# RWKV-7 recurrence and feed-forward: y's and the state's products as one of 104 columns

## The chip, the cores and the metric

The kernel runs on one core of a Trainium2 chip. What is measured is the device time of one launch in microseconds. All data is fp32.

The engines are called as the profile calls them: PE is TensorE's matmul, PEld its weight load, DVE is VectorE, ACT is ScalarE, POOL is GpSimd, SP is SyncE, which here issues nearly all DMA transfers.

## The reference

A linear recurrence over 768 steps for 4 batches of 8 heads, with a state of 40x40 for each head, and then a feed-forward block with a hard-swish:

```python
for t in range(S):                      # B, H, S, D = 4, 8, 768, 40
    y[:, :, t] = np.einsum('bhd,bhde->bhe', rt, state)
    Sa = np.einsum('bhde,bhe->bhd', state, at)
    state_decay = state * wt[:, :, None, :] - np.einsum('bhd,bhe->bhde', Sa, bt)
    state = state_decay + np.einsum('bhd,bhe->bhde', vt, kt)
...
x = attn_out.transpose(0, 2, 1, 3).reshape(B * S, H * D)     # 3072 x 320
h = x @ w_in                                                  # 320 x 2048
g = h * np.clip(h + 3.0, 0.0, 6.0) / 6.0
return g @ w_out                                              # 2048 x 320
```

The kernel takes the recurrence by blocks of 64 steps. Within a block the outputs come from the state at its start and from masked scores among its own steps; the correction Sa is found by inverting a triangular 64x64 matrix for each head.

## The kernel before

A *unit* is two batches by 64 steps by 8 heads; there are 24, numbered from 0. Units with even and odd numbers hold different batches, so unit i + 2 is the next that works on unit i's state. The 128 partitions hold two halves of 64: the two batches of a unit (q) or two heads (s). Four units form a group, for which VectorE inverts the triangular matrices in some 60 small steps (`invert`, L738 and L744).

A unit has two sets of stages. The *preparation* (`prepare`) needs no state: W and gam (running products of the decay), A, B, K (transposes and scaling), F (the matrix to invert), factor (scaled k and b, the tile KBt, held as `o["K"]` and `o["B"]`), E (masked scores of k and a) and EV (E times v). The unit's *own* stages (`step`) are:

- RT, VT: transposes of r and v; RT also scales the state by the decay
- R (L853): state times a, plus EV; S: transposes of the state; C: scores of v and r, masked
- U (L891), UT (L911): minus the inverse times R, as it is and transposed; rS (L927): the part of y from the old state, kept in ys
- sn (L946): the state's products, K's columns by v and B's columns by U, summed in PSUM, and then added to the state (L954, two instructions of VectorE); H: scores of U and r, masked
- y (L969): K's columns by C and B's columns by H, summed in PSUM, added to ys (L980), then multiplied by gam on POOL (L981, yg)
- move, move2: eight DMA transfers of yg into xt, the feed-forward's input

sn and y load the same columns of K and B as weights (40 of a head for sn, 64 for y). Each is 32 matmuls on quarters of the array, and each fp32 matmul leaves two records in the profile.

`masked` (L517) copies scores from PSUM into one of three score tiles through a 0/1 mask; the rest of such a tile stays zero. C, H and E take the three tiles in turn. U has a tile of its own, whose columns 40 to 63 of every head POOL clears for each unit (L868). That tile's place is also used by K1, an input tile of the odd units among the first eight.

The first four units follow a plan written by hand (`PLAN`). From unit 4 on the order is that of *blocks*, four to a unit: `OWN_STAGES` gives the own stages of unit i for the blocks from 4(i - 4) on, so its last two lists fall into the first two blocks of the next unit; `AHEAD_STAGES` or `CLOSE_STAGES` gives those of a unit whose preparation begins about five units earlier (`CLOSE_STAGES` where the next preparation begins less than four blocks later, units 8 to 11). `together` issues a block: first the TensorE products of all its stages, in the order of `PRODUCTS`, then what the other engines do with them, in the order of `RESULTS`. It counts PSUM banks as it goes (five to a batch); `WIDTH` gives the columns that a stage takes of a bank pair, and stages share a pair up to 512 columns. Feed-forward pieces (`feed`, `pieces`; L1051 and L1092 on TensorE, L1066 on ACT and L1067 on VectorE) and steps of the inversion (`aside`) come in between.

V is fetched into one of five tiles (L452, on SP's queue); the fetch waits for the last reader of the unit five before.

```python
OWN_STAGES = [["RT", "VT"], ["R", "C", "S"], ["U", "UT", "rS"], ["sn", "H"], ["y"],
              ["move", "move2"]]
AHEAD_STAGES = [["W", "gam"], ["A", "B"], ["F", "K"], ["E", "factor"], ["EV"]]
CLOSE_STAGES = [["W", "gam"], ["A", "B"], ["F", "K", "factor"], ["E"], ["EV"]]
```

Of the kernel before, what the change touches and what calls it, by code (L numbers as in the profile page):

```python
# [16 lines left out]
P = 128  # L17
BL = 64
HB = BL // 2
L = 32  # L20
SLOT = 64
EXP = 916

# [7 lines left out]
def kernel(  # L31
# [161 lines left out]
    def second(name):  # L193

        tag = {"B": "S", "K": "U"}[name]
        return padded(grp.tile([P, H, SLOT], F32, name=name + "1", tag=tag, bufs=1), name)

# [13 lines left out]
    for t in wms:  # L211
        nc.vector.memset(t[:], 0.0)
    inputs, others = {}, {}
    for name in "WABK":
# [4 lines left out]

    score = []  # L220
    for i in range(3):
        t = const.tile([P, H, BL], F32, name=f"score{i}")
        nc.gpsimd.memset(t[:], 0.0)
        score.append(t)
    turn = [0]
# [273 lines left out]
    def half(i, n=SLOT):  # L499
        return slice(SLOT * i, SLOT * i + n)  # L500

    def scores(lhs, rhs, swap=False):


        o = ps_pair(NPR, BL)
        for n in range(NPR):
            for q in range(2):
                for i in range(2):
                    nc.tensor.matmul(out=o[i][half(q), n, :],  # L509
                                     lhsT=lhs[half(i, D), n ^ (2 * q * swap), half(q)],  # L510
                                     rhs=rhs[half(i, D), n, half(q)], start=True, stop=True)
        return o

    def masked(o):
        turn[0] += 1
        x = score[turn[0] % len(score)]
        nc.vector.copy_predicated(out=x[:].rearrange("p (i h) t -> p i h t", i=2), mask=mask8, data=o[2])  # L517
        return x


    def prepare(i, F):
# [158 lines left out]
        def ev_stage():  # L680
# [8 lines left out]
            yield PE  # L689
            EV = grp.tile([P, 2, NPR, D], F32, name="EV", tag="EV")  # L690
            for x in range(2):
# [125 lines left out]
    def step(i):  # L817
# [47 lines left out]

        def new_U():
            U = m["U"] = grp.tile([P, H, SLOT], F32, name="U", tag="U", bufs=1)
            nc.gpsimd.memset(U[:, :, D:SLOT], 0.0)  # L868

        def s_S():  # L870

            sp = ps_any([P, 2, 2, P])
            for q in range(2):
                for j in range(2):
                    nc.tensor.transpose(out=sp[:, q, j, :],  # L875
                                        in_=st[:, q, 2 * j:2 * j + 2, :].rearrange("p r d -> p (r d)"),
                                        identity=ident[:])
            yield PE
            S = m["S"] = grp.tile([P, 2, 2, P], F32, name="S", tag="S", bufs=1)
            nc.scalar.activation(out=S[:], in_=sp[:], func=AF.Copy)  # L880
            new_U()

        def s_U():

            if fresh:
                new_U()
            up = ps_pair(NPR, D)
            for pr in range(NPR):
                for s in range(2):
                    for x in range(2):  # L890
# [3 lines left out]
            yield PE  # L894
            nc.scalar.activation(out=m["U"][:].rearrange("p (x r) d -> p x r d", x=2)[:, :, :, 0:D], in_=up[2],
                                 func=AF.Copy, scale=-1.0)

        def s_C():
            x = scores(m["VT"], m["RT"])
            yield PE  # L900
            m["K"] = masked(x)

# [33 lines left out]
        def s_sn():  # L936
            wide = SLOT if i < NU else D
            sn = ps_pair(NPR, D)
            for name in "KB":
                for pr in range(NPR):  # L940
                    for s in range(2):
                        for q in range(2):
# [3 lines left out]
                            nc.tensor.matmul(  # L946
                                out=sn[q][half(s, wide), pr, :],
                                lhsT=o[name][half(q), h * D:h * D + wide], rhs=by,
                                start=(name == "K" and pr == 0), stop=(name == "B" and pr == NPR - 1),
                            )  # L950
            yield PE
            for rows in [slice(0, P)] if i < NU else [half(s, D) for s in range(2)]:
                x = st[rows, :, :, 0:D]
                nc.vector.tensor_tensor(out=x, in0=sn[2][rows], in1=x, op=ALU.add)  # L954

        def s_H():
            x = scores(m["UT"], m["RT"], swap=True)
            yield PE
            m["B"] = masked(x)

# [37 lines left out]
        def s_move2():  # L998
            for dst, src in m["moves"][4:]:
# [5 lines left out]
                "rS": s_rS,  # L1005
                "sn": s_sn, "H": s_H, "y": s_y, "move": s_move, "move2": s_move2}

# [294 lines left out]
    for _ in range(18):  # L1302
# [6 lines left out]

    OWN_STAGES = [["RT", "VT"], ["R", "C", "S"], ["U", "UT", "rS"], ["sn", "H"], ["y"],  # L1310
                  ["move", "move2"]]
    AHEAD_STAGES = [["W", "gam"], ["A", "B"], ["F", "K"], ["E", "factor"], ["EV"]]
    CLOSE_STAGES = [["W", "gam"], ["A", "B"], ["F", "K", "factor"], ["E"], ["EV"]]


    PRODUCTS = ["W", "S", "K", "RT", "VT", "A", "B", "factor",
                "y", "EV", "R", "C", "U", "UT", "rS", "sn", "H", "E", "F"]
    RESULTS = ["RT", "y", "W", "VT", "EV", "R", "S", "C", "A", "B", "move", "move2",
               "U", "UT", "rS", "F", "K", "sn", "H", "E", "factor", "gam"]
    TURNS = PRODUCTS[:3]  # L1320
    WIDTH = {"R": NPR * D, "U": NPR * D, "sn": NPR * D, "EV": NPR * D}
    BLOCKS = 4
# [61 lines left out]
    def feed(n, inversion):  # L1384
# [5 lines left out]
        pieces(n - whole)  # L1390

    m = 0
    for i in range(NU, NK):
# [60 lines left out]
```

## Time and profile before

| | us |
|---|---|
| median of 3 runs | 800.2 |
| lowest and highest | 797.25, 800.67 |
| the profiled execution, device time | 800.17 |
| the profiled execution, span from first to last instruction | 798.4 |
| PE busy in the span | 734.0 |
| feed-forward on PE: L1051, L1092 | 252.6, 230.2 |
| sn on PE, L946 (both halves), 768 + 768 records | 14.4 + 14.0 |
| y on PE, L969 (last three places in PSUM), 1472 records | 27.4 |
| EV on PE, L687, 704 records | 14.9 |
| DVE state additions, L954, 44 | 21.4 |
| POOL clearings of U, L868, 24 of 0.256 | 6.1 |

The span is what the profile sees, from the first instruction to the last; the device time also holds what lies around it. A group of the profile is named by line, engine, operation, written and read tiles, and the sizes of both; its busy time is the union of its instructions, which overlap on PE. A line can be that of a helper: L509 is `scores`, called by E, C and H, and L517 is `masked`.

### The profile page before, as it was taken

To read this page: it belongs to the slowest core of one execution; us is meant where nothing else is said; L and a number is where in the kernel's file an instruction comes from. 1 tells how busy PE (TensorE), PEld (TensorE's weight loads), DVE (VectorE), ACT (ScalarE), POOL (GpSimd) and SP (SyncE) were. 2 spreads that over 40 slices of the span, in tenths; PEclk is the share of its full clock that TensorE was granted. 3 is DMA by queue.
4 is the path that set the end of the run, shared out by engine and by line. 5 is a ranking of instruction groups with operands and counts; after the bars stand their busy time and mean duration, and the time that the engine had idled before them with its cause. 6 is when DMAs were issued, how large, how long until landed. Compare 5 with 4: busy or idle time off the path is not lost.

```text
span 798.4 us, 35296 instructions
## 1 busy us (share of the span) xinstructions
PE 734.0 (92%) x15832; PEld 624.0 (78%) x15832; DVE 500.5 (63%) x986; ACT 307.1 (38%) x648; POOL 177.1 (22%) x318
## 2 busy tenths in 40 slices
PE   5726778999999989999999999999999999999998
PEld 4625667878778878788888888888888888888886
DVE  7898877689546699445798355888444983323210
ACT  2337653222553424452334454334444324412111
POOL 6403012421223313123214123304222202000000
PEclk9855798999999999999999999999999999999999
DMA  9693653420324322233212223213222101110000
GB/s 122 113 202 87 155 140 55 78 46 9 57 51 72 62 44 39 44 62 59 45 40 42 49 54 63 50 30 62 40 51 45 24 16 29 30 25 13 14 19 17
DMA packets 174214, 45.02 MB, mean 56 GB/s; under 512 B 157424, under 2 KB 172784, under 8 KB 174064
## 3 DMA queue, kind: packets, MB, share of 16 engines
q1 hardware_dynamic: 169760, 42.03, 27.8%
q8 instruction: 125, 2.05, 1.1%
q10 hardware_dynamic: 4304, 0.74, 0.7%
q14 instruction: 25, 0.20, 0.1%
HBM read 34.08 MB, written 3.93 MB: 48 GB/s over the span
## 4 chain that ended last, share of the span: by engine, by line
PE 77%; DVE 8%; issue 5%; SPq 5%; DMA 3%; ACT 1%; POOL 1%; POOLq 0%; DVEq 0%; ACTq 0%
PE h L1051 27%; PE o L1092 23%; PE pair L509 4%; PE pair L969 3%; SPq L455 3%; PE one L471 2%; PE pair L946 2%; PE pair L481 2%; PE pair L853 2%; PE pair L891 2%; PE pair L687 1%; PE pair L911 1%; PE pair L927 1%; PE one L875 1%; SPq L452 1%
## 5 line engine op out<-in xcount | busy, mean ns | idle before, releaser
L1051 PE MATMUL h<-xt,win 128*128 128x128 f32 (+1 forms) x2304 | 252.6, 284 | 3.2 <-DVE gt L1067 2.7
L1051 PEld LDWEIGHTS h<-xt,win 128*128 128x128 f32 (+1 forms) x2304 | 232.9, 193 | 20.6 <-issue 5.4
L1092 PE MATMUL o<-wout,gt 128*128 128x320 f32 x768 | 230.2, 443 | 0.0
L1092 PEld LDWEIGHTS o<-wout,gt 128*128 128x128 f32 x768 | 138.3, 190 | 50.2
L1067 DVE SCALAR_TENSOR_TENSOR gt<-gt,h 128x512 f32<-128x512 f32 x96 | 62.0, 682 | 71.2 <-ACT gt L1066 71.0
L1066 ACT ACTIVATE gt<-h,three 128x512 f32<-128x512 f32 x96 | 62.2, 686 | 101.6 <-PE h L1051 101.2
L981 POOL TENSOR_TENSOR yg<-ys,gam 128x512 f32<-128x512 f32 x22 | 39.7, 1803 | 162.6 <-DVE ys L980 71.8
L738 DVE TENSOR_TENSOR prod<-x 128x30 f32<-128x30 f32 (+9 forms) x180 | 67.2, 373 | 8.8 <-POOL x L723 3.3
L660 POOL TENSOR_TENSOR KBt<-K,rgt 128x320 f32<-128x320 f32 x22 | 19.1, 866 | 212.3 <-ACT rgt L649 207.4
L744 DVE TENSOR_TENSOR x<-x,prod 128x30 f32<-128x30 f32 (+9 forms) x180 | 62.3, 346 | 5.4
L954 DVE TENSOR_TENSOR state<-pair,state 40x320 f32<-40x320 f32 (+1 forms) x44 | 21.4, 487 | 65.5 <-PE pair L946 39.2
L517 DVE COPY_PREDICATED score<-mask,pair 128x512 f32<-128x512 int32 x71 | 50.0, 723 | 1.7 <-PE pair L509 1.2
L980 DVE TENSOR_TENSOR ys<-pair,ys 128x512 f32<-128x512 f32 x22 | 15.2, 690 | 40.9 <-PE pair L687 21.7
L552 DVE TENSOR_TENSOR_SCAN wm<-wm,start 128x528 f32<-128x528 f32 x24 | 37.6, 1566 | 0.8
L541 DVE TENSOR_TENSOR_SCAN prods<-wm,start 128x528 f32<-128x528 f32 x24 | 30.1, 1260 | 10.2 <-ACT wm L538 10.1
L831 ACT ACTIVATE RT<-pair 128x512 f32<-128x512 f32 x21 | 12.5, 597 | 52.8 <-PE pair L481 52.7
L692 ACT ACTIVATE EV<-pair 64x320 f32<-64x320 f32 x44 | 19.0, 432 | 33.7 <-PE pair L687 23.1
L806 ACT ACTIVATE tinv<-pair 32x256 f32<-32x256 f32 x48 | 18.0, 375 | 30.1 <-PE pair L796 29.4
L569 POOL COPY gam<-prods 128x256 f32<-128x256 f32 x24 | 22.5, 938 | 30.6 <-DVE prods L541 26.7
L1110 ACT ACTIVATE ob<-o 128x320 f32<-128x320 f32 x22 | 9.6, 435 | 49.4 <-PE o L1092 29.6
L969 PE MATMUL pair<-score,KBt 64*64 64x64 f32 x1472 | 27.4, 221 | 1.1 <-DVE state L954 0.9
L969 PEld LDWEIGHTS pair<-score,KBt 64*64 64x64 f32 x1472 | 24.0, 134 | 3.7 <-DVE state L954 1.4
(262 smaller groups left out, 1061.6 us busy)
## 6 DMA issues: line engine op xcount, KB each, us to landing
V<-in_v_dram SPq DMA_DIRECT2D x96, 40.0 KB
out_dram<-ob SPq DMA_DIRECT2D x47, 80.0 KB
R<-in_r_dram SPq DMA_DIRECT2D x92, 40.0 KB
B<-in_b_dram SPq DMA_DIRECT2D x42, 80.0 KB
K<-in_k_dram SPq DMA_DIRECT2D x42, 80.0 KB
W<-in_w_dram SPq DMA_DIRECT2D x37, 80.0 KB
A<-in_a_dram SPq DMA_DIRECT2D x37, 80.0 KB
xt<-yg SPq DMA_DIRECT2D x72, 40.0 KB
```

Source lines behind the costliest of these rows:

```text
L509: nc.tensor.matmul(out=o[i][half(q), n, :], lhsT=lhs[half(i, D), n ^ (2 * q * swap), half(q)], rhs=rhs[half(i, D), n, half(q)], start=True ...
L517: nc.vector.copy_predicated(out=x[:].rearrange("p (i h) t -> p i h t", i=2), mask=mask8, data=o[2])
L541: nc.vector.tensor_tensor_scan(out=prods[:].rearrange("p r m i -> p (r m i)"), data0=wm[:, 0:SCAN], data1=start[:], initial=0.0, op0=ALU.m ...
L552: nc.vector.tensor_tensor_scan(out=back, data0=back, data1=start[:], initial=0.0, op0=ALU.mult, op1=ALU.add)
L738: nc.vector.tensor_tensor(out=pv, in0=_ap(x[:], (i + 1) * L + i, [[L, n], [0, i]]), in1=_ap(x[:], i * L, [[0, n], [1, i]]), op=ALU.mult,)
L744: nc.vector.tensor_tensor(out=rest, in0=rest, in1=pv, op=ALU.add)
L969: nc.tensor.matmul(out=y[q][half(s), pr, :], lhsT=o[name][half(q), h * D:h * D + SLOT], rhs=m[name][half(q), 4 * rs + 2 * s + j, :], start ...
L981: nc.gpsimd.tensor_tensor(out=yg[:], in0=m["ys"][:].rearrange("p r q t -> p r (q t)"), in1=o["G"][:], op=ALU.mult)
L1051: nc.tensor.matmul(out=hp[c][:, i, :], lhsT=lhsT, rhs=rhs, start=(begun[c] == 0), stop=(begun[c] == 3 * NQ - 1))
L1066: nc.scalar.activation(out=gt[:], in_=hp[c][:], func=AF.Relu, bias=three[:], scale=1.0)
L1067: nc.vector.scalar_tensor_tensor(out=gt[:], in0=gt[:], scalar=6.0, in1=hp[c][:], op0=ALU.min, op1=ALU.mult)
L1092: nc.tensor.matmul(out=op[:], lhsT=gts[c][:, n, :], rhs=wout[:, c * HJ + r * NQ + n, :], start=((split or r == 0) and c == 0 and n == 0), ...
```

## The change

From unit 4 on, sn is no longer a stage of its own. y's products get a moving operand of 104 columns: 64 of masked scores and, beside them, 40 of v (for K's columns) or of U (for B's). The result holds y in its first 64 columns and the state's products in the other 40; VectorE adds the first to ys, then the second to the state. Two views of a new tile `store` hold the operands: `by_v` and `by_u`. C's and H's masks are written into them, ACT writes U beside H, and a new stage, beside, copies v beside C by a DMA transfer from SBUF to SBUF on SP's queue. H's scores are taken in another order of heads, so that H and U stand in the same order.

Three slots of `store` serve the first four units as score tiles and as the place of U and K1; U's columns 40 to 63 are no longer cleared for each unit. From unit 4 on only one score tile is left, for E. EV moves from the block after E to four blocks after E (two in `CLOSE_STAGES`), and has four slots instead of five.

```diff
+    store = const.tile([P, 2 * H * BOTH], F32, name="store")
+    slots = [store[:, n * H * BL:(n + 1) * H * BL].rearrange("p (h t) -> p h t", h=H) for n in range(3)]
+    by_v, by_u = (store[:, n * H * BOTH:(n + 1) * H * BOTH].rearrange("p (h t) -> p h t", h=H) for n in range(2))
...
-    score = []
-    for i in range(3):
-        t = const.tile([P, H, BL], F32, name=f"score{i}")
-        nc.gpsimd.memset(t[:], 0.0)
-        score.append(t)
+    score = [const.tile([P, H, BL], F32, name="score")[:], slots[0], slots[1]]
+    for t in score:
+        nc.gpsimd.memset(t, 0.0)
...
-    def scores(lhs, rhs, swap=False):
+    def scores(lhs, rhs, swap=False, back=False):
...
-                                     rhs=rhs[half(i, D), n, half(q)], start=True, stop=True)
+                                     rhs=rhs[half(i, D), n ^ (2 * q * back), half(q)],
+                                     start=True, stop=True)
...
+    def masked_beside(o, x):
+        nc.vector.copy_predicated(out=x[:, :, 0:BL].rearrange("p (h i) t -> p i h t", i=2), mask=mask8, data=o[2])
+        return x
...
-            EV = grp.tile([P, 2, NPR, D], F32, name="EV", tag="EV")
+            EV = grp.tile([P, 2, NPR, D], F32, name="EV", tag="EV", bufs=NU)
...
-        def new_U():
-            U = m["U"] = grp.tile([P, H, SLOT], F32, name="U", tag="U", bufs=1)
-            nc.gpsimd.memset(U[:, :, D:SLOT], 0.0)
...
+            m["U"] = by_u[:, :, BL:] if halves else slots[2][:, :, 0:D]
...
-            m["K"] = masked(x)
+            m["K"] = masked_beside(x, by_v) if halves else masked(x)
...
+            x = scores(m["UT"], m["RT"], swap=not halves, back=halves)
+            yield PE
+            m["B"] = masked_beside(x, by_u) if halves else masked(x)
+
+        def s_beside():
+
+            nc.sync.dma_start(out=by_v[:, :, BL:], in_=VN[:, :, 0:D])
+            yield from ()
+
+        def s_y_sn():
+
+            y = ps_pair(NPR, BOTH)
+            for name in "KB":
+                for pr in range(NPR):
+                    for s in range(2):
+                        for q in range(2):
+                            h = 2 * pr + s
+                            x = 4 * s + pr if name == "K" else 4 * (s ^ q) + pr
+                            nc.tensor.matmul(
+                                out=y[q][half(s), pr, :],
+                                lhsT=o[name][half(q), h * D:h * D + SLOT], rhs=m[name][half(q), x, :],
+                                start=(name == "K" and pr == 0), stop=(name == "B" and pr == NPR - 1))
+            yield PE
+            yg = m["yg"] = tmp.tile([P, NPR, P], F32, name="yg", tag="yg", bufs=2)
+            x = m["ys"][:].rearrange("p r q t -> p q r t")
+            nc.vector.tensor_tensor(out=x, in0=y[2][:, :, :, 0:BL], in1=x, op=ALU.add)
+            nc.gpsimd.tensor_tensor(out=yg[:], in0=m["ys"][:].rearrange("p r q t -> p r (q t)"),
+                                    in1=o["G"][:], op=ALU.mult)
+            for s in range(2):
+                x = st[half(s, D), :, :, 0:D]
+                nc.vector.tensor_tensor(out=x, in0=y[2][half(s, D), :, :, BL:], in1=x, op=ALU.add)
...
-    OWN_STAGES = [["RT", "VT"], ["R", "C", "S"], ["U", "UT", "rS"], ["sn", "H"], ["y"],
+    OWN_STAGES = [["RT", "VT"], ["R", "C", "S", "beside"], ["U", "UT", "rS"], ["H"], ["y"],
                   ["move", "move2"]]
-    AHEAD_STAGES = [["W", "gam"], ["A", "B"], ["F", "K"], ["E", "factor"], ["EV"]]
-    CLOSE_STAGES = [["W", "gam"], ["A", "B"], ["F", "K", "factor"], ["E"], ["EV"]]
+    AHEAD_STAGES = [["W", "gam"], ["A", "B"], ["F", "K"], ["E", "factor"], [], [], [], ["EV"]]
+    CLOSE_STAGES = [["W", "gam"], ["A", "B"], ["F", "K", "factor"], ["E"], [], ["EV"]]
...
-    WIDTH = {"R": NPR * D, "U": NPR * D, "sn": NPR * D, "EV": NPR * D}
+    WIDTH = {"R": NPR * D, "U": NPR * D, "y": NPR * BOTH, "EV": NPR * D}
...
+    for t in (by_v, by_u):
+        nc.gpsimd.memset(t[:, :, 0:BL], 0.0)
+    del score[1:]
```

`PRODUCTS` and `RESULTS` lose sn; beside stands last but one in `RESULTS`, so a block issues its transfer behind move and move2. `BOTH` is 104.

## The prediction

> **What bounds the kernel now.** I read the page first, then busy time in stretches of the span, then TensorE's timeline in one unit, and last TensorE's waits.
>
> ```profile
> PE 734.0 (92%) x15832; PEld 624.0 (78%) x15832; DVE 500.5 (63%) x986; ACT 307.1 (38%) x648; POOL 177.1 (22%) x318
> PE   5726778999999989999999999999999999999998
> PE 77%; DVE 8%; issue 5%; SPq 5%; DMA 3%; ACT 1%; POOL 1%; POOLq 0%; DVEq 0%; ACTq 0%
> ...
> 0.00:215.00 215.00, 161.45 (x3461) 139.16 (x3462) 171.91 (x349) 90.82 (x177) 57.21 (x123) 0.84 0.50 98
> 215.00:305.00 90.00, 86.04 (x2010) 71.89 (x2010) 60.91 (x127) 36.20 (x87) 21.73 (x40) 1.00 0.30 54
> 305.00:655.00 350.00, 347.02 (x7956) 297.09 (x7955) 230.70 (x452) 142.72 (x315) 87.17 (x137) 1.00 0.25 46
> 655.00:756.00 101.00, 101.00 (x2164) 84.85 (x2166) 31.18 (x51) 31.57 (x61) 9.70 (x18) 1.00 0.10 22
> ```
>
> The last four lines are stretches: length, then busy time of PE, PEld, DVE, ACT, POOL, then granted clock, DMA share and GB/s. The units that the change touches (the fifth on, 20 of 24) run from about 200 us to 756 us. There TensorE is idle for 4.0 us before 305, 3.0 us to 655 and nothing to 756, at a clock of 1.00; some 4 us more are lost behind 756, where only the feed-forward is left. So in these units a microsecond of TensorE work is a microsecond of the kernel, and the other engines count only where they make TensorE wait: 7 us in all. The first 215 us (first four units and the weights) have TensorE at 75%, and the change barely touches them.
>
> Now one unit on TensorE (start, length, line, operands, count):
>
> ```profile
> 522.85 0.68 PE L853 MATMUL pair<-state,at 40*64 40x40 f32 x32
> 523.34 0.67 PE L509 MATMUL pair<-RT,VT 40*64 40x64 f32 x32
> ...
> 538.69 0.51 PE L946 MATMUL pair<-V,KBt 64*40 64x40 f32 x32
> 539.02 0.55 PE L946 MATMUL pair<-U,KBt 64*40 64x40 f32 x32
> 539.40 0.69 PE L509 MATMUL pair<-RT,UT 40*64 40x64 f32 x32
> ...
> 548.41 1.16 PE L969 MATMUL pair<-score,KBt 64*64 64x64 f32 x64
> 549.39 0.63 PE L687 MATMUL pair<-V,score 64*64 64x40 f32 x32
> 549.95 2.05 PE L1051 MATMUL h<-xt,win 128*128 128x128 f32 x16
> ```
>
> Lengths overlap, so I take start to start. Each product has two records. The state's products (L946) take 0.33 + 0.38 = 0.71 us for 64 records, y's (L969) 0.98 us for 64: 1.69 us a unit. All use quarter tiles (64 rows by 64 or 40 columns), four at a time.
>
> **The change, part by part.**
>
> 1. *Products.* Gone: 64 records with 40 weight columns and 40 moving columns. Grown: 64 records from 64 to 104 moving columns, weights as before. A record of y costs 0.98/64 = 15.3 ns, one of the state's 0.33/32 = 10.3 ns; the 24 columns between make 5.0 ns, or 0.21 ns a column. (L853, 40 moving columns on 64 weight columns, costs 0.49/32 = 15.3 ns, as much as 64 on 64: the longer of load and stream sets the step, not their sum.) So 104 columns cost 15.3 + 40 x 0.21 = 23.7 ns, 64 of them 1.52 us; saved 0.17 us. What follows takes part of it back. y is now followed by a 128-wide feed-forward tile where EV stood; in the late units, where that is so already, y takes 1.09 instead of 0.98 us. So +0.11 on y, and -0.07 on EV (0.56 us ahead of h now, 0.49 us as L853 ahead of another small product). That leaves 0.13 us in the 13 units with a unit ahead; in the seven without, 0.33 + 0.31 + 1.09 = 1.73 against 1.63, or 0.10 us. Sum: 13 x 0.13 + 7 x 0.10 = 2.4 us; I take 2.2, since a stop of 0.07 us ahead of H (0.38 against 0.31 us in the late units) may now fall on EV. No row has 104 columns on quarter tiles. Lower end of their price: 104 x 0.21 = 21.8 ns with no fixed part, 1.40 us, a gain of 4.6 us over 20 units. Upper end: two tiles at a time instead of four, 43.7 ns, 2.80 us, a loss of 20 us. The nearest rows, quarter tiles of the same weights, go four at a time, and I take that.
>
> The Trainium skill, "TensorE: Matmul & The Clock Gate", Part 1 ("Wait — 56ns, not 53.3ns?"), puts a floor of about 25 ns start to start under every small matmul. By it the 64 records gone would be worth 1.6 us a unit, an estimated 32 us in all; the trace's 10.3 ns a record says that quarter tiles side by side are under no such floor here, and I go by the trace. The same page, Part 3 ("The mechanism"), says that a weight load overlaps running matmuls only where the row group differs, which speaks against the change: two of each four tiles share rows. The trace's 15.3 ns a record for tiles with shared rows leaves no place for loads that do not overlap.
>
> 2. *EV, three blocks later* (one block later where units are prepared three blocks apart). Its products and its two evictions are the same. What goes is its wait for E's mask, which VectorE makes just before:
>
> ```profile
> 289.86 0.40 DVE L744 TENSOR_TENSOR x<-x,prod 128x228 f32<-128x228 f32 x1
> 290.18 0.48 DVE L857 TENSOR_TENSOR RR<-pair,EV 128x320 f32<-128x320 f32 x1
> 290.58 0.71 DVE L517 COPY_PREDICATED score<-mask,pair 128x512 f32<-128x512 int32 x1
> ...
> 291.39 0.68 PE L687 MATMUL pair<-V,score 64*64 64x40 f32 x32 [1.50 <-issue]
> ...
> PE pair L853 <- DVE score L517: 1.0, 1, 1.0
> PE pair L687 <- PE pair L481: 1.0, 1, 1.0
> ```
>
> VectorE works off the inversion (L738, L744), the mask comes at 291.3, and EV starts right behind it after 1.50 us. A second EV waits 1.0 us, near 244. A block of slack, some 6 us (24.5 us a unit over four blocks), covers both: -2.5 us. Bounds: 0, if VectorE's lateness meets the next product of TensorE that needs it; -3.5, if R's wait (L853, 1.0 us, for the PSUM pair that E's mask frees) goes too. EV's slots drop from five to four; a slot is written at block 7 and last read at block 21 of its unit, 14 of 16 blocks, so nothing waits. E's only score tile is written in the block where the EV before has just read it, and EV's products stand ahead of E's: no new wait.
>
> 3. *y alone in its PSUM pair.* ys (0.69 us) no longer waits for EV's products in the same banks (0.96 us at 550.09), nor EV's eviction for ys. Off TensorE's path: 0, between -0.5 (xt earlier; h waited 0.5 us for xt once) and 0.
>
> 4. *The state's two additions* (0.49 us each) leave the block of H and E and come after ys, ahead of W's scans. VectorE's total is the same; H's and E's masks come 0.98 us earlier, the scans later by as much. The next unit works on the other state, and the same state is scaled four blocks on: 0 on the path, covered by the 7 us of TensorE work from y (548.4) to the next unit's R (555.9), the first that takes y's banks again. Without that cover it is rival 2.
>
> 5. *The copy of v beside the scores*: 20 transfers of 128 x 8 = 1,024 runs of 160 B. The queue moved 169,760 packets in 27.8% of 16 x 798.4 us, 20.9 ns each, so one transfer is 64 x 20.9 ns = 1.3 us on all 16 engines; share 0.25 to 0.31 or so. SP issues it in about 0.6 us (V's fetches: 616 ns in the median), behind the eight moves of the unit before. It waits for y's products one block back, done by then; queued behind it are output writes and, two blocks on, V, B and K. It must land before y, three blocks (18 us) later. 0; if SP were blocked, the 18 us would have to be used up first.
>
> 6. *V free earlier.* V's last reader is now this transfer, not the state's product, so the waits of V's fetch for L946 go (79.1 us in 12 waits on SP's queue). B and K follow sooner. TensorE waits for none of them behind 215 us: 0.
>
> 7. *POOL*: 24 clearings of U at 0.26 us go, two of 128x512 come once (0.5 to 1 us each, by 0.26 us for 192 columns). POOL is 22% busy: 0, between -1 and +1 in the first four units, where it queued 14.0 us behind U's readers in three waits.
>
> Masks, U and the sums now step by 104 elements instead of 64 or 40; sizes are the same, and VectorE's state add already reads PSUM in runs of 40 at 488 ns: 0.
>
> Sum: -2.2 - 2.5 = -4.7 us against the profiled execution's 800.17 us (span 798.4, and 1.8 around it): 795.5 us. The runs shown have a median of 800.2, from 797.25 to 800.67, so the same number stands against the median: -0.6%.
>
> **Rivals.**
>
> 1. *The waits form anew* (no change): the products gain their 2.2 us, but VectorE, with the inversion in its queue at 277 to 292 us, is late for the next product instead of for EV. For it: R's wait of 1.0 us there, same cause. Against: feed-forward tiles stand between, and from 305 on they hide almost everything. 800.2 - 2.2 = 798.0.
> 2. *VectorE's move bites* (slower): the state's additions stand ahead of the scans and of the feed-forward's second eviction (L1067) in the block after H. In 519.6 to 546 VectorE, with the inversion, is idle for 1.3 us of 26. If five such stretches, one per group of four units, each pass 0.98 us on to TensorE and the waits of EV only move, that is +4.9 - 2.2: 802.9. It decides once h's waits for gt (2.7 us now) exceed about 5 us. Against: the same 0.98 us leaves the block just before.
> 3. *More idle time goes*: R's wait and half of the 4 us left also vanish, as E and EV are apart and rgt no longer waits for the state's addition in its bank (36.3 us of ACT): -2.2 - 3.5 - 2 = 792.5.
> 4. *Two tiles at a time*: +1.11 us a unit, +22 - 2.5: 820. Against: every 64-row, 64-column row above.
>
> **How the numbers follow.** Forecast 0.46, rival 1 0.28, rival 2 0.13, rival 3 0.10, rival 4 0.03. About 0.5% (4 us) is what a measurement of this kernel can tell from no change. The forecast lies 0.7 us beyond that line, so some 0.32 of its 0.46 is faster, and 0.14 within; with rival 3 and a little of rival 1: faster 0.46. Within: 0.14 + 0.24 = 0.38 or so. Slower: rivals 2 and 4 = 0.16. The range goes from rival 3 less a microsecond of the product's lower price, 791, to rival 2, 802.5; the forecast's own range is 793 to 797.5.
>
> **What would show it.** 64 records of one line a unit, 1.5 us start to start (1.4 to 1.6; 2.8 for rival 4); EV between the factor's transposes and H, with no idle time ahead of it; TensorE idle for about 4.5 us from 215 to 655 instead of 7; no wait of y for the copy of v; SP's wait for L946 gone. The forecast is wrong if h's waits for gt grow, if the idle time near 280 stands ahead of another product, or if the first 215 us move by more than 2 us.

## The result and the profile after

The changed kernel takes 794.21 us in the median of six runs (793.32 to 794.59), against 798.69 us for six runs of the kernel before: a ratio of 0.9943, with a 95% interval of 0.9924 to 0.9961. A second measurement gave 0.9934 (0.9917 to 0.9951), 793.42 us. The profiled execution took 794.59 us, with a span of 792.9 us, 5.5 us below the 798.4 us of before.

The page and the stretches of the changed kernel (the columns are those of before):

```profile
PE 727.6 (92%) x14552; PEld 615.8 (78%) x14552; DVE 496.8 (63%) x986; ACT 307.1 (39%) x648; POOL 161.5 (20%) x296
...
0.00:215.00 215.00, 160.27 (x3496) 137.31 (x3500) 172.47 (x349) 92.08 (x180) 56.77 (x120) 0.86 0.52 98
215.00:305.00 90.00, 87.83 (x1867) 72.69 (x1857) 62.80 (x137) 36.30 (x84) 19.89 (x36) 1.00 0.34 61
305.00:655.00 350.00, 345.68 (x7079) 294.72 (x7077) 229.94 (x448) 142.86 (x316) 76.19 (x127) 1.00 0.29 51
655.00:756.00 101.00, 101.00 (x1920) 84.66 (x1919) 27.79 (x48) 30.73 (x60) 8.68 (x14) 1.00 0.14 29
```

TensorE is as full as before (92%), with 1,280 records fewer. The first 215 us look alike. From 215 to 305 us its idle time fell from 4.0 to 2.2 us; from 305 to 655 us it *rose* from 3.0 to 4.3 us. So the gain isn't simply less of everything. The two traces stand side by side by the begin of U's products (L891 before, L893 after) of each unit; the feed-forward issues the same number of records between any two of these marks in both kernels, so the difference is that of the recurrence alone:

```
                                   before    changed
begin of unit 4's U products       210.5     209.1     -1.4
from there to unit 23's            532.5     528.4     -4.1
  of it small products             186.3     182.7     -3.6
  of it TensorE idle                 8.1       7.7     -0.4
from unit 23's to the end           55.4      55.4      0.0
```

The idle time behind unit 4's mark, by what ended it (gaps over 0.1 us):

```
                                              before    changed
EV, two waits                                   2.46      0
h for gt, in three blocks                       0.64      2.80
R for E's mask, near 284 us                     1.02      1.01
L620/L628 for ACT's ys, near 213 us             1.21      1.21
the inversion's products for wm, twice          0.50      0.50
in units 5 to 7: R and the inversion, three     0         0.86
h for xt                                        0.46      0
no releaser, EV's left out                      1.77      1.14
```

EV's waits went, and h's waits for gt grew by nearly as much.

Then one block with the inversion, TensorE and VectorE from y's products (start, length, engine, line, operands; in brackets the idle time before and what ended it). In the changed kernel:

```profile
506.77 1.66 PE L975 MATMUL pair<-store,KBt 64*64 64x104 f32 x64
508.36 1.16 PE L1079 MATMUL h<-xt,win 128*128 128x128 f32 x8
508.50 0.69 DVE L982 TENSOR_TENSOR ys<-pair,ys 128x512 f32<-128x512 f32 x1 [1.40 <-PE pair L975]
509.11 0.98 DVE L987 TENSOR_TENSOR state<-pair,state 40x320 f32<-40x320 f32 x2
509.36 4.47 PE L1120 MATMUL o<-wout,gt 128*128 128x320 f32 x16
510.12 1.54 DVE L549 TENSOR_TENSOR_SCAN prods<-wm,start 128x528 f32<-128x528 f32 x1
...
511.99 1.32 DVE L560 TENSOR_TENSOR_SCAN wm<-wm,start 128x528 f32<-128x528 f32 x1
...
513.95 1.29 DVE L1095 SCALAR_TENSOR_TENSOR gt<-gt,h 128x512 f32<-128x512 f32 x2
514.78 1.13 PE L1079 MATMUL h<-xt,win 128*128 128x128 f32 x8 [0.95 <-DVE gt L1095]
```

and from the same block in the kernel before:

```profile
514.24 0.69 DVE L980 TENSOR_TENSOR ys<-pair,ys 128x512 f32<-128x512 f32 x1 [0.73 <-PE pair L687]
514.85 1.25 DVE L541 TENSOR_TENSOR_SCAN prods<-wm,start 128x528 f32<-128x528 f32 x1
...
518.96 1.27 DVE L1067 SCALAR_TENSOR_TENSOR gt<-gt,h 128x512 f32<-128x512 f32 x2
...
519.77 1.13 PE L1051 MATMUL h<-xt,win 128*128 128x128 f32 x8 [0.20 <-DVE gt L1067]
```

Two things are to be seen. The 64 records with 104 columns take 508.36 - 506.77 = 1.59 us, with a 128-wide tile behind them. And VectorE's row from ys to gt is one chain: the state's additions now stand in it, gt begins 5.45 us behind ys instead of 4.72, and h waits 0.95 us for it instead of 0.20. This happens in three blocks, at 279, 397 and 514 us (0.90, 0.95, 0.95 us; before 0.23, 0.21, 0.20).

### The profile page after: what moved, and what is told of

It reads as the page before. It is cut to its first block, busy times and chain, and to the rows that moved or that the text cites. A ratio compares the mean times of both kernels' runs of the same rounds, so it can differ in the third digit from the quotient of the medians.

```text
span 792.9 us, 32747 instructions
## 1 busy us (share of the span) xinstructions
PE 727.6 (92%) x14552; PEld 615.8 (78%) x14552; DVE 496.8 (63%) x986; ACT 307.1 (39%) x648; POOL 161.5 (20%) x296
## 3 DMA queue, kind: packets, MB, share of 16 engines
HBM read 34.08 MB, written 3.93 MB: 48 GB/s over the span
## 4 chain that ended last, share of the span: by engine, by line
PE 76%; DVE 10%; issue 4%; DMA 3%; SPq 2%; ACT 2%; POOL 1%; DVEq 0%; POOLq 0%; ACTq 0%
PE h L1079 26%; PE o L1120 24%; PE pair L512 4%; PE pair L975 4%; PE one L474 2%; PE pair L484 2%; PE pair L893 2%; PE pair L861 2%; PE pair L695 1%; DVE wm L560 1%; DVE prods L549 1%; PE pair L929 1%; PE pair L913 1%; DVE prod L746 1%; DVE x L752 1%
## 5 line engine op out<-in xcount | busy, mean ns | idle before, releaser
L746 DVE TENSOR_TENSOR prod<-x 128x30 f32<-128x30 f32 (+9 forms) x180 | 65.0, 361 | 9.0 <-POOL x L731 3.5
L525 DVE COPY_PREDICATED store<-mask,pair 128x512 f32<-128x512 int32 x40 | 29.0, 725 | 62.6 <-PE pair L512 62.5
L668 POOL TENSOR_TENSOR KBt<-K,rgt 128x320 f32<-128x320 f32 x19 | 16.4, 865 | 204.5 <-ACT rgt L657 184.4
L983 POOL TENSOR_TENSOR yg<-ys,gam 128x512 f32<-128x512 f32 x20 | 25.5, 1273 | 147.5 <-DMA R<-in_r_dram 69.6
L549 DVE TENSOR_TENSOR_SCAN prods<-wm,start 128x528 f32<-128x528 f32 x24 | 33.5, 1401 | 10.7 <-ACT wm L546 10.2
L975 PE MATMUL pair<-store,KBt 64*64 64x104 f32 x1280 | 33.1, 252 | 0.0
L560 DVE TENSOR_TENSOR_SCAN wm<-wm,start 128x528 f32<-128x528 f32 x24 | 31.1, 1297 | 0.8
L975 PEld LDWEIGHTS pair<-store,KBt 64*64 64x64 f32 x1280 | 29.1, 133 | 1.5
L865 DVE TENSOR_TENSOR RR<-pair,EV 128x320 f32<-128x320 f32 x21 | 10.3, 489 | 23.7 <-PE pair L512 20.5
L897 ACT ACTIVATE store<-pair 128x320 f32<-128x320 f32 x24 | 10.5, 437 | 37.0 <-PE pair L913 33.6
```

The costliest lines, as they stand in the source:

```text
L525: nc.vector.copy_predicated(out=x[:, :, 0:BL].rearrange("p (h i) t -> p i h t", i=2), mask=mask8, data=o[2])
L549: nc.vector.tensor_tensor_scan(out=prods[:].rearrange("p r m i -> p (r m i)"), data0=wm[:, 0:SCAN], data1=start[:], initial=0.0, op0=ALU.m ...
L560: nc.vector.tensor_tensor_scan(out=back, data0=back, data1=start[:], initial=0.0, op0=ALU.mult, op1=ALU.add)
L746: nc.vector.tensor_tensor(out=pv, in0=_ap(x[:], (i + 1) * L + i, [[L, n], [0, i]]), in1=_ap(x[:], i * L, [[0, n], [1, i]]), op=ALU.mult,)
L975: nc.tensor.matmul(out=y[q][half(s), pr, :], lhsT=o[name][half(q), h * D:h * D + SLOT], rhs=m[name][half(q), x, :], start=(name == "K" and ...
L983: nc.gpsimd.tensor_tensor(out=yg[:], in0=m["ys"][:].rearrange("p r q t -> p r (q t)"), in1=o["G"][:], op=ALU.mult)
```

## The experiments

Twelve kernels ran. All but the repeat of the kernel before start from the changed kernel. Each was timed against the kernel before on the same chip; that kernel's median was between 797.9 and 799.2 us.

**The changed kernel again.**

> The changed kernel once more, as the measure for the others of this job: 794 us (793.3 to 794.6 in six runs). Theory: TensorE idles 0.90, 0.95 and 0.96 us behind the feed-forward's second eviction (h waits for gt) in three blocks of the inversion, at about 279, 397 and 513 us, at the same places again. Rival (these gaps are chance of one execution): they lie elsewhere or are shorter than 0.4 us.

It took 793.42 us, with gaps of 0.91, 0.95 and 0.95 us at 279, 397 and 513 us. They are no chance. "Begin of unit 4's U products" and so on below are compared with this execution: 208.7 us, then 527.2 us to unit 23's, 7.2 us of it idle.

**y and the state's products apart again.**

```diff
-            for name in "KB":
-                for pr in range(NPR):
+            for part, wide in ((slice(0, BL), SLOT), (slice(BL, BOTH), D)):
+                for name in "KB":
+                    for pr in range(NPR):
...
-                                lhsT=o[name][half(q), h * D:h * D + SLOT], rhs=m[name][half(q), x, :],
+                                    lhsT=o[name][half(q), h * D:h * D + wide], rhs=m[name][half(q), x, part],
```

> The changed kernel, but y and the state's products are 64 matmuls again instead of 32, in the same block, the same banks and from the same operands (64 columns with 64 weight columns, then 40 columns with 40). Nothing else differs. Theory (joining them saves TensorE time): start to start 0.98 + 0.33 + 0.31 us, and 0.1 for the h behind it, 1.70 instead of 1.59 us a unit, +0.11 x 20 = 2.2 us over the changed kernel, 796.4 us. Rival (the gain is in the order of stages alone): no difference, 794.2 us. Second rival (pieces with 64 rows pay for every record): over +5 us.

It took 801.75 us, ratio 1.0042 (1.0026 to 1.0058): 8.3 us more than the changed kernel and more than the kernel before. The products took 1.71 instead of 1.59 us where no gap fell into them, as expected: 0.12 x 20 = 2.4 us. The other 6 us were not expected. From one unit's U products to the next, the profiled execution is some 0.12 us slower nearly everywhere, and 0.4 to 1.2 us slower in seven places (behind units 5, 12, 15, 16, 17, 20 and 21). In five of these seven TensorE has a gap with nothing to wait for, as here in unit 17:

```profile
598.25 0.41 PE L484 MATMUL pair<-ident,V 64*128 64x64 f32 x8
598.59 1.71 PE L976 MATMUL pair<-store,KBt 64*64 64x64 f32 x121
601.16 0.28 PE L976 MATMUL pair<-store,KBt 64*40 64x40 f32 x7 [0.85 <-issue]
```

"issue" means that no releaser is to be found, and the gap falls in the middle of a row of products with the same operands. The page has a DMA queue of kind "instruction", which moves blocks of 16 KB: 125 of them in the kernel before and in this one, 115 in the changed one. By the kernel before, 2 x 15,832 records of PE and PEld in 125 blocks, a block is some 253 of TensorE's records (an estimate). The ends of these gaps (those over 0.5 us behind 250 us) against the last block that had begun to load:

```
gap ends at     273.81  457.24  511.16  546.93  576.45  601.16
load began at   271.2   454.7   508.7   544.7   574.0   598.6
```

Each time 2.2 to 2.6 us lie between the two. That speaks for TensorE having run out of instructions; no run shows it outright. Not every such gap costs its length: units 6 and 14, with those that end at 273.81 and 511.16, are only 0.01 and 0.21 us slower, since h waits less for gt behind them. The next kernel asks whether the dense row of products is what uses them up.

**A feed-forward piece between the two halves.**

```diff
             for part, wide in ((slice(0, BL), SLOT), (slice(BL, BOTH), D)):
+                if wide == D and next(stream):
+                    owed[0] -= 1
```

> As two_products (y and the state's products as 64 matmuls in one block; 801.8 us), but with one feed-forward piece of 128-wide tiles between the two halves, taken from those that come behind, so that no more than 64 of these matmuls stand in a row. Theory (two_products lost some 5 us because 256 instructions of matmul and weight load in 1.7 us are used up faster than a block of 256 instructions, 16 KB, is loaded; its idle gaps with nothing to wait for ended 2.2 to 2.6 us behind the begin of such a load): those gaps shrink; changed kernel 793.8 + 2.4 for the products + some 2 for one more change of tile shape a unit = 798 us. Rival (the gaps have another cause, which stays): 803 us or more.

It took 808.17 us, ratio 1.0122 (1.0097 to 1.0147): a miss. The extra changes of tile shape cost 0.34 and 0.33 us in units 18 and 22, where nothing waits (against two_products), and gaps without a releaser were still there, only elsewhere: six between 228 and 584 us, 0.46 to 1.03 us long, ending 2.2 to 3.4 us behind the begin of a load. So breaking up the dense row does not take them away. That the changed kernel, with fewer instructions, has fewer such gaps (1.1 and 0.5 us in its two profiles, against 4.6 in two_products) is what the runs show. The number of instructions isn't all of it, as the kernel before, with as many blocks as two_products, has only 1.8 us of them; the mechanism stays open.

The rest of this kernel's loss can be read from the trace. From unit 4's to unit 23's U products it takes 7.6 us more than two_products: 0.8 us of idle time, 2.2 of small products and 4.7 of the feed-forward, whose records are the same. Of the 4.7, 2.6 lie in units 5 and 6. There the granted clock is 0.50 for 3.4 us twice, from 251.7 and from 289.2 us, right behind waits of 1.03 and 0.65 us and of 1.97 us; in the kernel before and in the changed one it is 1.00 all through these units.

**EV right behind E again, in units 8 to 11.**

```diff
-    CLOSE_STAGES = [["W", "gam"], ["A", "B"], ["F", "K", "factor"], ["E"], [], ["EV"]]
+    CLOSE_STAGES = [["W", "gam"], ["A", "B"], ["F", "K", "factor"], ["E"], ["EV"]]
```

> The changed kernel, but where units are prepared three blocks apart (units 8 to 11) EV stands in the block right after E again, as before the change. Theory (EV was late because its mask on VectorE was): the waits of 0.96 and 1.50 us ahead of EV come back near 242 and 285 us, +2.5 us, 796.7 us. Rival (the state's addition that stood ahead of E's mask was what made EV wait, and it is gone): EV waits less than 0.5 us, 794.5 us.

It took 793.81 us, ratio 0.9945 (0.9925 to 0.9965), next to 793.42 us. EV's waits are back, 0.51 us at 241 and 1.50 us at 288:

```profile
286.93 0.48 DVE L865 TENSOR_TENSOR RR<-pair,EV 128x320 f32<-128x320 f32 x1
287.33 0.71 DVE L525 COPY_PREDICATED store<-mask,pair 128x512 f32<-128x512 int32 x1
...
288.14 0.68 PE L695 MATMUL pair<-V,score 64*64 64x40 f32 x32 [1.50 <-issue]
```

but most of the time isn't: unit 6 to 7 takes 36.18 instead of 34.08 us, and unit 7 to 8 takes 30.36 instead of 31.87. Of these differences 0.7 and 0.6 us are EV's own products, which fall into the other stretch; idle time makes up +1.1 and -0.7 us. While 2.0 us of waits came back at EV, four others shrank or went: h's near 279 us from 0.91 to 0.50 us, R's in unit 5 (0.17) and the inversion's in unit 7 (0.36 and 0.38), 1.3 us together. VectorE, with the inversion in its queue, is late there as a whole, and of the wait that one product is spared, most falls to others. The move of EV in these units is worth some 0.6 us at the begin of unit 8, not 2.5. That holds for the changed kernel; with the state's additions in their old place it was not tried. Undoing the steady units' move (EV four blocks behind E) was not tried either.

**The state's additions behind the feed-forward pieces.**

```diff
-            for s in range(2):
-                x = st[half(s, D), :, :, 0:D]
-                nc.vector.tensor_tensor(out=x, in0=y[2][half(s, D), :, :, BL:], in1=x, op=ALU.add)
+            def add():
+                for s in range(2):
+                    x = st[half(s, D), :, :, 0:D]
+                    nc.vector.tensor_tensor(out=x, in0=y[2][half(s, D), :, :, BL:], in1=x, op=ALU.add)
+            late.append(add)
```

(`late` is worked off in `a_block` behind the first half of the block's feed.)

> The changed kernel, but the two additions to the state are issued to VectorE behind the first half of the block's feed-forward pieces instead of right behind ys. Theory (the additions stand ahead of the scans and of gt and cost 0.7 us in each of three blocks with the inversion): h's gaps of 0.90, 0.95 and 0.96 us shrink to some 0.2, -2.2 us, 792.0 us. Rival (VectorE is short of time there and the wait only goes to the next product): the gaps at these places shrink, as much idle time appears behind them, 794.2 us. Second rival: y's banks are held longer and the next block's products wait for them, 795 us or more.

It took 820.4 us, ratio 1.027 (1.025 to 1.029). The second rival, and more of it than expected: y's PSUM pair stays taken until the additions, and the next block's R needs it.

```profile
499.22 1.27 DVE L1098 SCALAR_TENSOR_TENSOR gt<-gt,h 128x512 f32<-128x512 f32 x2
500.41 0.98 DVE L988 TENSOR_TENSOR state<-pair,state 40x320 f32<-40x320 f32 x2
501.54 1.09 PE L861 MATMUL pair<-state,at 40*64 40x40 f32 x32 [3.03 <-DVE state L988]
```

The additions now stand behind gt, which itself waits for TensorE. h no longer waits for gt, but R waits for the additions, three times for 1.8 to 3.0 us. TensorE is idle for 19.9 us behind 200 us, instead of 7.4. That is not half of the loss; the rest is the clock. TensorE behind the wait shown (PE, PEld, DVE, ACT, POOL, granted clock, DMA share, GB/s):

```profile
501.50:508.20 6.70, 6.66 (x73) 5.00 (x74) 2.31 (x5) 0.00 (x0) 0.00 (x0) 0.50 0.19 40
508.50:525.00 16.50, 16.50 (x324) 14.30 (x323) 10.28 (x21) 6.74 (x16) 3.75 (x10) 1.00 0.15 28
```

There are six such stretches at 0.50 behind unit 4, of 3.4 or 6.8 us, 30.7 us together, each beginning between 1.0 us ahead of and 1.7 us behind the end of a gap of 1.7 to 3.0 us. From unit 4's to unit 23's U products this kernel takes 27.8 us more than the changed one: 12.6 us of idle time and 15.1 us in which the same products take longer (11.4 of them in the feed-forward, in the six units with these stretches), next to 30.7 / 2 = 15.4 us for half the clock. So TensorE's gaps here cost more than twice their length.

**The additions on ACT and POOL.**

```diff
-            for s in range(2):
-                x = st[half(s, D), :, :, 0:D]
-                nc.vector.tensor_tensor(out=x, in0=y[2][half(s, D), :, :, BL:], in1=x, op=ALU.add)
+            sums = by_v[:, :, BL:].rearrange("p (q r) d -> p q r d", q=2)
+            nc.scalar.activation(out=sums, in_=y[2][:, :, :, BL:], func=AF.Copy)
+            for s in range(2):
+                x = st[half(s, D), :, :, 0:D]
+                nc.gpsimd.tensor_tensor(out=x, in0=sums[half(s, D)], in1=x, op=ALU.add)
```

> The changed kernel, but VectorE no longer adds the products to the state: ACT copies them out of PSUM (one instruction, into v's columns of the operand, free by then) and POOL adds them. Theory (0.98 us of VectorE's queue ahead of the scans and of gt cost 0.7 us in each of three blocks): h's gaps of 0.9 us at 279, 397 and 513 us shrink to 0.2, and nothing holds y's banks longer: -2 us, 791.7 us. Rival (the wait goes on to the next product there): no difference, 793.8 us. Second rival (ACT's or POOL's queue is longer than VectorE's, as with the late addition): 797 us or more.

It took 796.52 us, ratio 0.9970 (0.9954 to 0.9986), and h's gaps *grew* to 1.30, 1.35 and 1.35 us: the second rival. ACT's copy waits for ys and holds up W's copies behind it in ACT's queue, so that VectorE waits 1.10 us for the first scan (`DVE L549`, released by ACT's wm): it starts 1.79 us behind ys, no earlier than with the additions ahead of it (1.62). POOL's two additions, 3.59 us together at 511.5, hold up POOL's copies behind them, and beside them VectorE's own copy into gam (L573) takes 0.75 us instead of 0.28. So gt begins 5.86 us behind ys instead of 5.45. The next kernel issues both steps later:

```diff
+            m["sn"] = y[2][:, :, :, BL:]
+
+        def s_out():
+            sums = m["sums"] = by_v[:, :, BL:].rearrange("p (q r) d -> p q r d", q=2)
+            nc.scalar.activation(out=sums, in_=m["sn"], func=AF.Copy)
+            yield from ()
+
+        def s_add():
             for s in range(2):
                 x = st[half(s, D), :, :, 0:D]
-                nc.vector.tensor_tensor(out=x, in0=y[2][half(s, D), :, :, BL:], in1=x, op=ALU.add)
+                nc.gpsimd.tensor_tensor(out=x, in0=m["sums"][half(s, D)], in1=x, op=ALU.add)
+            yield from ()
...
-    RESULTS = ["RT", "y", "W", "VT", "EV", "R", "S", "C", "A", "B", "move", "move2",
-               "U", "UT", "rS", "F", "K", "H", "E", "factor", "beside", "gam"]
+    RESULTS = ["RT", "y", "W", "VT", "out", "EV", "R", "S", "C", "A", "B", "move", "move2",
+               "U", "UT", "rS", "F", "K", "H", "E", "factor", "beside", "gam", "add"]
```

> As add_pool (796.5 us; ACT copies the state's products out, POOL adds), but ACT's copy is issued behind W's copies and VT, and POOL's additions behind gam, as add_pool held W's copies 1.1 us in ACT's queue and gam's some 3.5 us in POOL's. Theory (0.98 us of VectorE ahead of gt cost 0.7 us in three blocks): the gaps of h shrink from 0.95 to below 0.3, -2 us, 791.8 us. Rival (whatever leaves VectorE, the next product waits): 793.8 us or more.

It took 791.61 us, ratio 0.9922 (0.9900 to 0.9945). In the block shown above h now waits 0.20 us, at 398 us as well, and near 279 us 0.17:

```profile
508.41 0.69 DVE L982 TENSOR_TENSOR ys<-pair,ys 128x512 f32<-128x512 f32 x1 [1.42 <-PE pair L975]
509.01 1.25 DVE L549 TENSOR_TENSOR_SCAN prods<-wm,start 128x528 f32<-128x528 f32 x1
...
513.12 1.27 DVE L1104 SCALAR_TENSOR_TENSOR gt<-gt,h 128x512 f32<-128x512 f32 x2
...
513.93 1.13 PE L1088 MATMUL h<-xt,win 128*128 128x128 f32 x8 [0.20 <-DVE gt L1104]
```

The scan starts right behind ys. R's wait for E's mask near 283 us grew from 1.0 to 1.6 us, the lateness passed on there. Behind it the granted clock is 0.50 for 3.4 us, from 285.6 us, and unit 6 takes 35.54 us instead of 34.08. The ratio's interval overlaps the changed kernel's (0.9917 to 0.9951), so here too the gaps are the better evidence.

**W's first scan ahead of ys.**

```diff
-    RESULTS = ["RT", "y", "W", "VT", "EV", "R", "S", "C", "A", "B", "move", "move2",
+    RESULTS = ["RT", "W", "y", "VT", "EV", "R", "S", "C", "A", "B", "move", "move2",
```

> The changed kernel, but in a block VectorE gets W's first scan ahead of ys and the state's additions. Theory (VectorE idles 1.4 us for y's products at these places, and then ys, additions, scans and gt run one behind the other): the scan fills the idle time, h's gaps of 0.9 us at 278, 397 and 513 us become 0.2 to 0.5, -1.5 us, 792.3 us. Rival (the wait goes on): 793.8 us.

It took 792.84 us, ratio 0.9929 (0.9917 to 0.9940), with gaps of 0.57, 0.24 and 0.24 us: the scan runs in VectorE's idle time ahead of ys. The gain over the changed kernel, some 0.6 us in the median, is within the spread of its runs; the gaps in the trace are the better evidence.

**Both together.**

> The two that shortened h's wait for gt, together: ACT and POOL add the products to the state (add_split, 791.6 us) and W's first scan goes ahead of ys (w_first, 792.8 us). Theory (both take from the same three gaps, of which 0.2 us are left): no more than 0.5 us below add_split, 791 us. Rival (the idle time left near 280 us, R's wait for E's mask, shrinks too): 790 us.

It took 791.03 us, ratio 0.9918 (0.9887 to 0.9949), the fastest of all, within 0.6 us of add_split alone. Its four runs (790.48 to 791.61) all lie below the fastest of the changed kernel's twelve (792.31). R's wait near 284 us is 1.59 us in it, and no stretch at half the clock follows.

**The transfer twice.**

```diff
-            nc.sync.dma_start(out=by_v[:, :, BL:], in_=VN[:, :, 0:D])
+            for _ in range(2):
+                nc.sync.dma_start(out=by_v[:, :, BL:], in_=VN[:, :, 0:D])
```

> The changed kernel, but each transfer of v beside the scores is issued twice (the same bytes to the same place). Theory (it lies behind other work): the same as the changed kernel, 793.8 us, with 20 more transfers of 1,024 runs. Rival (SP's queue or the DMA engines pass it on): 0.6 to 1.3 us for each of 20, up to +20 us.

It took 796.53 us, ratio 0.9972 (0.9957 to 0.9987): 2.6 us more than clear_u, measured beside it (793.97), not nothing. The test was not the clean doubling I meant: the two issues stretch over 4.04 us of SP's queue where a single one takes 0.68, so the second waited, apparently for the first to land in the same place. Behind it the next fetches of V, B and K came late, and TensorE waited for B:

```profile
232.31 4.04 SPq L964 DMA_DIRECT2D store<-V  x2
236.39 3.71 SPq L455 DMA_DIRECT2D V<-in_v_dram  x4
240.21 1.29 SPq L458 DMA_DIRECT2D B<-in_b_dram  x2
...
243.84 0.70 PE L484 MATMUL pair<-ident,B 64*128 64x64 f32 x8 [1.40 <-DMA B<-in_b_dram]
```

Of the 5.4 us that this execution lost up to unit 23's U products, 3.2 lie between units 5 and 6: this wait, and behind it 3.4 us at a granted clock of 0.50 (from 245.0 us), which cost some 1.7 us. From unit 6 to unit 17 the stretches agree with the changed kernel's within 0.3 us, although TensorE waits 0.83 us for W near 273 us and the two issues take 3.6 us or more in each unit. So SP's queue has some 3 us to give in a steady unit, and none around unit 5. The single transfer costs TensorE no wait: behind 205 us the changed kernel's trace has none for a DMA.

**The kernel before again, and U's clearing put back.**

> The kernel before once more: 798.3 us. If the gain ahead of the fifth unit belongs to the change (U's R on TensorE, L891/L893, of unit 4 at 208.5 to 209.4 us in four profiles with the change, 210.5 us in the one before), unit 4's comes at 210 us or later again; if that was chance, at 209 us or earlier.

It took 798.47 us, and unit 4's U products began at 211.0 us.

```diff
             nc.scalar.activation(out=S[:], in_=sp[:], func=AF.Copy)
+            if not halves:
+                nc.gpsimd.memset(slots[2], 0.0)
...
+            if fresh:
+                nc.gpsimd.memset(slots[2], 0.0)
             m["U"] = by_u[:, :, BL:] if halves else slots[2][:, :, 0:D]
```

> The changed kernel, but POOL clears U's place for each of the first four units again, behind the last readers of U. Theory (the clearing held POOL, and behind it yg and the moves into xt, in the first units): unit 4 reaches its U stage 1 to 2 us later and the whole is 795 us. Rival (POOL's wait there was not on the path): 793.8 us, the same as the changed kernel.

It took 793.97 us, with unit 4's mark at 207.9 us: the rival. The clearing is not what the first units gained. Their gain is there in all profiles: 210.5 and 211.0 us without the change, 207.9 to 209.8 us in twelve with it. Part of it goes with the clock, which is 0.50 for 68 and 65 us ahead of this mark without the change and for 55 to 65 us with it; but the two profiles with the change that have 65 us as well stand at 209.4 and 209.8 us, still over 1 us earlier. Where it comes from stays open. The four units' products are the same in both; score tiles, U's place and EV's slots differ, and which of them counts was not tried.

## Why the prediction was right, and where

The total, 795.5 us against 800.2 shown, or -4.7 us, was right: the measured difference of the medians is 4.5 us, that of the profiled executions 5.6 us. It was made of other parts than the sum had, and that it came so close is in part luck: between the profiled executions the small products gave -3.6 us (forecast -2.2), the idle time -0.4 (forecast -2.5) and the first four units -1.4 (forecast 0), and these errors of -1.4, +2.1 and -1.4 us cancel for the most part.

Two of the prediction's own signs of being wrong came. h's waits for gt grew, from 2.7 to 4.9 us in the whole span, close to the 5 us at which rival 2 was to decide; and near 280 us idle time stands ahead of another product, h instead of EV. TensorE's idle time from 215 to 655 us is 6.5 us (6.0 in the second execution), not 4.5. The other signs held: 1.59 us for the 64 records, no idle time ahead of EV, no wait of y for the copy of v, and SP's wait for the state's product gone.

1. *Products*, -2.2 us predicted: too small. The record's price held: 104 columns cost 24.8 ns with the 128-wide tile's share in it, forecast 23.7 plus 1.7 ns; 40 columns more cost 1.59 - 1.09 = 0.50 us over 64 records, 0.19 ns a column, forecast 0.21. Four tiles run abreast, rival 4 is out. Undoing the join alone cost 2.4 us of products, what was forecast for all of it. The gain a unit was mis-sized, 0.13 us where a unit is ahead. y with its 128-wide tile took 1.59, not 1.63 us; the stop of 0.07 us ahead of H did not come (EV took 0.49 us, H behind it 0.49); and E's records, 0.61 us before, took 0.58. Units without idle time show the whole: 32.42 to 32.23 us for unit 18, 24.64 to 24.52 for unit 22, 0.19 us with a unit ahead and 0.12 without. Over 20 units, at 0.19 for some 15 and 0.12 for 5, that is an estimated 3.5 us, and the table's small products give 3.6.

2. *EV later*, -2.5 us predicted: this step failed by its size. Both waits went, as forecast, but the idle time fell by 0.4 us only (1.0 in the second execution). That small fall is not this step's alone: 2.2 us came with the additions (point 3), 0.9 us stand newly in units 5 to 7, and 1.1 us less of gaps without a releaser and of h's wait for xt go the other way. What the step itself is worth shows in ev_close: with 2.0 us of EV's waits back, 1.3 us of other waits went, and the time stayed within 0.4 us. So rival 1 had it right for units 8 to 11, and so had the bound of 0 that the prediction gave for this term. The error was to add up the gaps ahead of one product, where the engine that caused them, VectorE with the inversion in its queue, was late for others as well.

3. *The state's additions*, 0 predicted: wrong. Rival 2's mechanism is there, at three places instead of five and for 0.7 us each, 2.2 us in all, too little to turn the sign (rival 2 had 0.98 us in each of five). I had covered the move with the 7 us between y and the next R, that is, with when the *results* are needed. What counted was what stands *behind* the additions in VectorE's queue: the scans, then gt, then h. add_split, which takes them out of the queue, brought all three gaps down to 0.2 us; w_first, which fills the idle time ahead of it, did so for two and left 0.57 us at the third.

4. *The transfer* and *V's earlier release*, 0 predicted: held, as far as tried. SP's waits for the state's product (79.1 us) are gone; V's fetch now waits for the transfer instead, 27.1 us in 12 waits, and TensorE does not feel it.

5. *The first four units*, -1 to +1 us predicted, -1.4 us in the first pair of profiles and some 2 us over all: outside, and not by the mechanism I named.

Two readings of the prediction were off without consequence: a unit takes 28.0 us in the mean between units 4 and 23 (532.5 / 19), not 24.5, and rival 2's sum is 802.9, where the range ends at 802.5.

## What to carry to other kernels

When one saturated engine sets the time, count its instructions by what a row of them costs start to start, and take the price of a longer operand from the difference of two rows: here that was right to 10%. Before a small step is moved in an engine's queue, look at what then stands behind it and who waits for that, not only at when its own result is needed. Idle time ahead of one product is worth its length only if the engine that causes it is not late for the next one as well. And a longer gap can cost more than its length: look at the granted clock behind it before the loss is put down to waiting alone.

## What the hardware showed that I had not expected

TensorE has gaps without any releaser that end a short time after a 16 KB block of its instructions began to load. In the fourteen profiles there are 30 over 0.25 us behind 205 us (EV's left out), up to 1.03 us long, and all of them end 2.2 to 3.4 us after such a begin, where the blocks begin 5.4 to 6.3 us apart in the median. Two kernels that differ by 1,280 matmul records and 0.12 us of products a unit differed by 8.3 us, and 4.5 us of the 7.2 us that their profiled executions differed by up to unit 23 lie in the five stretches that hold such a gap, beyond 0.12 us each.

The granted clock fell to 0.50 for 3.4 or 6.8 us at every gap of TensorE of 1.6 us or more behind unit 4 (eight in add_late, two_apart and add_split, between 1.60 and 3.03 us). Below that it did so behind one of 1.40 us (beside_twice) and behind a pair of 1.03 and 0.65 us (two_apart), and not behind gaps of 1.50 us (the kernel before, add_late, ev_close) and 1.59 us (add_split_w). So these runs give no sharp threshold.

POOL's addition of 40x320 took 1.69 to 1.83 us in the 24 places where VectorE's scans ran beside it (all in add_pool) and 0.85 to 1.01 us in the 56 others (16 in add_pool, 40 in add_split).
